# Attention and two feed-forward layers on one core: the last 512 tokens of the first phase in one group, and instruction order from a table

## The chip, the cores and the metric

The kernel runs on one core of one Trainium2 chip. The metric is the device time of one execution in microseconds (us). Five engines work from lists of their own and wait for each other by semaphores: TensorE (PE; its weight loads are shown apart as PEld), VectorE (DVE), ScalarE (ACT), GpSimd (POOL), and SyncE (SP), whose queue issues the transfers from and to memory.

## The reference

```python
scores = (1.0 / np.sqrt(D)) * np.matmul(q, k.transpose(0, 1, 3, 2))      # 2 batches, 8 heads, 768 tokens, head 64
keep = is_global | is_local                                              # first 8 tokens, or 0 <= rel < 96
scores = np.where(keep, scores + bias, -1000000000.0)                    # bias: -slope of the head * distance
a = np.exp(scores - np.max(scores, axis=-1, keepdims=True))
x = np.matmul(a / (np.sum(a, axis=-1, keepdims=True) + 1e-09), v)        # then to (1536 tokens, 512)

h = x @ moe_w_in;  x = (np.maximum(h, 0.0) + np.log1p(np.exp(-np.abs(h)))) @ moe_w_out    # 512 -> 2048 -> 512
h = x @ moe2_w_in; x = (h * np.clip(h + 3.0, 0.0, 6.0) / 6.0) @ moe2_w_out                # 512 -> 2048 -> 512
```

The weights come as 64-bit words.

## The kernel before

**Attention.** Tokens are worked on in 12 blocks of 128. A quad is half a block: four heads. Each of the 24 quads goes through scores on TensorE (`att_s`, L512, into tiles `s`), bias and minimum on VectorE (L543), exponential and row sum on ScalarE (L548), the reciprocal on VectorE (L429, L430), normalising on GpSimd (L432), eight 128x128 transposes on TensorE (`att_t`, L571, into `ptp`), copies to SBUF on ScalarE (L573, `pT`), and value matmuls on TensorE (`att_v`, L589, into `px`). Two quads make a block; then ScalarE and VectorE split the result into a high and a low part, `xsh` (L596) and `xsl` (L597). The first block of a batch has no block to its left, and its two quads have scores of 128 and not of 256 columns, half the transposes and half the value matmuls; they are called narrow here.

**The layers.** Each layer has 16 chunks of 128 hidden units, in phases of 6, 5 and 5 chunks. A chunk's product with x, the activation, and the product with the second weight matrix, summed up over a phase's chunks, are done for a group of tokens at a time. Every product is three matmuls (high by low, low by high, high by high; `matmul3`, L209). Outside the first phase a group has 512 tokens (`item`, L277: 12 matmuls into `h`, 12 into `acc`). In the first phase of the first layer, which runs beside attention, an item is a pair of chunks by 256 tokens (`first_h`, `first_o`, `first_end`; L228 to L275): a half item of 24 matmuls into `hf`, the activation (`split_g`, L184, with the tiles `t`, `ghf`, `glf`), and a half item of 24 into `accf`. There are 6 token groups of 256 and 3 pairs, so 18 items and 36 half items; `first_items` (L220) gives their order. All matmuls of the layers stand on L214.

**Weights.** A unit is half a chunk's weights (512 KB). `unit_load` (L106) loads it; `unit_convert` (L119) makes 32-bit high and low parts: from unit 12 on absolute value on ScalarE (L137) and clamp on GpSimd (L140), then always a shift (L141) and two merges (L146, L147) on VectorE, a rounding copy on ScalarE (L151), and a subtraction on VectorE (L152). The first phase uses 6 chunks, units 0 to 11. When attention is through, its memory becomes five more chunk slots (`grow`, L85), and units 12 and up are converted.

**What sets the order.** TensorE's order is written out by `run` (L368): `half` puts attention's steps in front of certain matmuls of a half item (before the first, before the thirteenth or twenty-second), and every TensorE instruction is kept in program order (`ordered`, L364). The first instruction of a unit's conversion is kept in program order too (L139, L145). All else on the other engines and the SP queue is placed by a scheduler that works with the estimated times of a simulated timeline when the program is built. Ahead of the first item TensorE does 24 warm-up matmuls (`warm_up`, L680).

Of the kernel before, what the change touches and what calls it, by code (L numbers as in the profile page):

```python
# [53 lines left out]

class Layers:
# [6 lines left out]
    def __init__(self, ctx, tc, weights, three, xsh, xsl, out):  # L62
# [14 lines left out]
        self.room, self.hint, self.bare = None, False, 0  # L77
        self.n_h, self.halves, self.in_first, self.beside = 0, 0, True, False
# [27 lines left out]
    def unit_load(self, x):  # L106
        j, u = self.order[x]
        layer, f = divmod(j, NCH)
        z = self.home(x, 5)
        if z < 2:  # L110
            raw = self.part[1][:, 2 * z:2 * z + 2, :].rearrange("p m t -> p (m t)").bitcast(I32)
            raw = raw.rearrange("p (c t) -> p c t", t=2)
        else:
            pool = self.room if z == 4 else self.wr[x % len(self.wr)]
            raw = pool.tile([P, CW, 2], I32, tag="raw", name=f"raw{j}_{u}")
        self.nc.sync.dma_start(out=raw.rearrange("p c t -> p (c t)"), in_=self.weights[2 * layer + u][f])
        self.raws[x] = raw

    def unit_convert(self, x):  # L119
# [16 lines left out]
        if not bare:  # L136
            first = nc.scalar.activation(a, raw.bitcast(F32)[:, :, 1], AF.Abs)  # L137
            if self.in_first:
                self.tc.keep_in_program_order(first)  # L139
            nc.gpsimd.tensor_scalar(out=a, in0=a, scalar1=W_HI, scalar2=W_LO, op0=ALU.min, op1=ALU.max)  # L140
        first = nc.vector.tensor_scalar(  # L141
            out=ai, in0=hi if bare else ai, scalar1=3, scalar2=0x3FFFFFF8, op0=ALU.logical_shift_left, op1=ALU.bitwise_and
        )
        if bare:
            self.tc.keep_in_program_order(first)  # L145
        nc.vector.scalar_tensor_tensor(out=ai, in0=hi, scalar=-2 ** 30, in1=ai, op0=ALU.bitwise_and, op1=ALU.bitwise_or)  # L146
        nc.vector.scalar_tensor_tensor(  # L147
            out=ai, in0=lo, scalar=29, in1=ai, op0=ALU.logical_shift_right, op1=ALU.bitwise_or
        )
        wh, wl = self.W[j][2 * u:2 * u + 2]  # L150
        nc.scalar.copy(wh, a)  # L151
        nc.vector.tensor_tensor(out=wl, in0=a, in1=r32(wh), op=ALU.subtract)  # L152
# [31 lines left out]
    def split_g(self, layer, hf, n, where=None):  # L184
# [4 lines left out]
        t3 = self.tp.tile([P, 512], F32, tag="t", name=f"t3{n}")  # L189
        if layer == 0:  # L190
            t2 = self.tp.tile([P, 512], F32, tag="t", name=f"t2{n}")
            nc.scalar.activation(t1, hf, AF.Abs)
            nc.scalar.activation(t1, t1, AF.Exp, scale=-1.0)
            if self.beside:
                nc.gpsimd.tensor_scalar(out=t2, in0=t1, scalar1=1.0, scalar2=1.0, op0=ALU.mult, op1=ALU.add)
            else:
                nc.scalar.add(t2, t1, 1.0)
            nc.scalar.activation(t3, t2, AF.Ln)
            nc.vector.scalar_tensor_tensor(out=t2, in0=t2, scalar=-1.0, in1=t1, op0=ALU.add, op1=ALU.subtract)  # L199
            nc.vector.scalar_tensor_tensor(out=t3, in0=hf, scalar=0.0, in1=t3, op0=ALU.max, op1=ALU.add)  # L200
            nc.vector.tensor_tensor(out=t3, in0=t3, in1=t2, op=ALU.subtract)
# [3 lines left out]
        nc.scalar.copy(gh, t3)  # L205
        nc.vector.tensor_tensor(out=gl, in0=t3, in1=r32(gh), op=ALU.subtract)  # L206
# [13 lines left out]
    def first_items(self):  # L220
# [4 lines left out]
        runs += [(g, EARLY_PAIRS, n) for g in range(EARLY)] + [(g, 0, n) for g in range(EARLY + 1, T // GT)]  # L225
# [38 lines left out]
    def first_end(self, i):  # L264
        g, s, _, last, more = self.items[i]
        G, o = divmod(g * GT, GB)
        if last:
            for z in range(2):
                pm = self.part[G][:, 2 * z:2 * z + 2, o:o + GT]
                if more:  # L270
                    self.nc.vector.tensor_tensor(out=pm, in0=self.acc[z], in1=pm, op=ALU.add)
                else:
                    self.nc.scalar.copy(pm, self.acc[z])
        if g == T // GT - 1:
            self.release(0, 0, (2 * s, 2 * s + 1))  # L275
# [88 lines left out]
    def ordered(self, call):  # L364

        self.tc.keep_in_program_order(call())

    def run(self, att=None, spare_step=lambda: None):  # L368
# [19 lines left out]
        grown = False  # L388
        ahead, z = [], 0
        for i in range(n):  # L390
            if not grown and (att is None or att.done()):
                if att:
                    att.close()
                    self.beside, self.room = False, None
                self.grow(1, MORE_SLOTS, 2, 2)
                grown = True
# [4 lines left out]
            self.first_end(i)  # L401
        self.in_first = False
# [24 lines left out]
def softmax_rows(nc, sm, rs, pm):  # L427

    nc.vector.tensor_scalar(out=rs, in0=sm, scalar1=EPS, scalar2=None, op0=ALU.add)  # L429
    nc.vector.reciprocal(out=rs, in_=rs)  # L430
    for j, t in enumerate(pm):
        nc.gpsimd.tensor_scalar(out=t, in0=t, scalar1=rs[:, j:j + 1], scalar2=0.0, op0=ALU.mult, op1=ALU.add)  # L432


def fast_path(tc, ident, three, nf, counts, q, k, qt, kt, v, weights, out, flag):


    with ExitStack() as ctx, ExitStack() as actx:
# [4 lines left out]
        layers.bare = 2 * PHASES[0][0]  # L443
        tp = layers.tp
# [37 lines left out]
        nc.gpsimd.iota(rel[:, 2, :], pattern=[[-1, P]], base=0, channel_multiplier=1, **iota)  # L482
        nc.gpsimd.iota(gc[:, 2, :], pattern=[[1, P]], base=0, channel_multiplier=0, **iota)
        nc.gpsimd.iota(rel[:, 1, :], pattern=[[-1, P]], base=P, channel_multiplier=1, **iota)
        nc.vector.memset(gc[:, 0:2, :], BIG)
        nc.vector.tensor_scalar(out=far[:, 2, :], in0=rel[:, 2, :], scalar1=0.0, scalar2=BIG, op0=ALU.is_lt, op1=ALU.mult)
        nc.vector.tensor_tensor(out=rel[:, 2, :], in0=rel[:, 2, :], in1=far[:, 2, :], op=ALU.add)
        nc.vector.tensor_copy(rel[:, 0, :], rel[:, 2, :])
        nc.vector.memset(rel[:, 1, 0:MAX_GLOBAL], BIG)
        nc.vector.tensor_copy(gc[:, 1, 0:MAX_GLOBAL], gc[:, 2, 0:MAX_GLOBAL])  # L490
        counts()
        ng, nl = nf[:, 0:1], nf[:, 1:2]

        nc.vector.tensor_scalar(out=gfar, in0=gc, scalar1=ng, scalar2=BIG, op0=ALU.is_ge, op1=ALU.mult)
        nc.vector.tensor_scalar(out=far, in0=rel, scalar1=nl, scalar2=BIG, op0=ALU.is_ge, op1=ALU.mult)
        nc.vector.tensor_tensor(out=far, in0=far, in1=rel, op=ALU.add)
        nc.vector.scalar_tensor_tensor(out=far, in0=gfar, scalar=nl, in1=far, op0=ALU.add, op1=ALU.min)
        for h in range(H):
# [13 lines left out]
        def att_s(k):  # L512
# [3 lines left out]
            if e == 0:  # L516
# [3 lines left out]
                if i == 0:  # L520
                    nc.scalar.copy(gk, kT[:, :, slot, 0:MAX_GLOBAL])
# [19 lines left out]
            for z in range(4):  # L541
                pmz = pm[:, z, 0:w]
                nc.vector.tensor_tensor_reduce(  # L543
# [3 lines left out]
                )  # L547
                nc.scalar.activation(pmz, pmz, AF.Exp, bias=nm[:, z:z + 1], scale=-1.0, accum_out=sm[:, z:z + 1])  # L548
# [326 lines left out]
```

## Time and profile before

| | |
|---|---|
| median of 3 runs | 631.61 us (631.17 to 632.33) |
| the profiled execution: time | 630.09 us |
| the profiled execution: span of its instructions | 628.3 us |
| TensorE busy | 613.8 us, 98% |
| VectorE, ScalarE, GpSimd busy | 71%, 60%, 21% |
| memory read and written | 56.10 MB, 3.15 MB |

The profiler records one execution. The span goes from its first to its last instruction; the 1.8 us around it belong to the time of the execution. Times in rows count from the start of the span. A matmul's recorded end is modelled and overlaps the next one's start, so what one costs in a row of many is read from the distance of the starts, or from the time of a group in the chain. The chain that ended last is followed back from the last instruction, at each step to what released it.

### The profile page before, as it was taken

Reading aid. Unit: us, or ns where it says so; the run is one execution under the profiler, and the core shown is the slowest. Engines: PE = TensorE matmul, PEld = TensorE weight load, DVE = VectorE, ACT = ScalarE, POOL = GpSimd, SP = SyncE. Lnnn points to the kernel's source line nnn. Section 1 sums busy time; section 2 is a strip of 40 time slices with the busy share of each in tenths; the row PEclk is TensorE's granted clock in tenths of the full one; section 3 lists DMA queues with packets and bytes.
Section 4 is the critical chain, followed back from the end, with each engine's and each line's share of the span. In section 5 each row is a group of like instructions: output and inputs, shape, how many; then the busy total and the mean of one; then the engine's idle time right before and its main releaser. Section 6 shows DMA issues by size and latency. Waiting matters only on the chain.

```text
span 628.3 us, 9717 instructions
## 1 busy us (share of the span) xinstructions
PE 613.8 (98%) x3495; PEld 514.8 (82%) x3496; DVE 448.8 (71%) x945; ACT 375.3 (60%) x796; POOL 132.0 (21%) x168
## 2 busy tenths in 40 slices
PE   8898999999999999999999999999999999999997
PEld 4587878899999888877788888888888888888886
DVE  7995687635799999999998996224999633424262
ACT  6986888774778887776788852425455742222130
POOL 3474353430132233533301410000100000000000
PEclk9998999999999999999999999999999999999999
DMA  8763312101144343333401143001457620001011
GB/s 278 272 196 106 106 39 69 35 14 68 68 133 137 96 139 119 123 107 117 140 34 57 45 135 101 1 1 33 142 191 233 207 67 1 1 0 68 1 67 69
DMA packets 26804, 59.91 MB, mean 95 GB/s; under 512 B 2688, under 2 KB 9344, under 8 KB 26752
## 3 DMA queue, kind: packets, MB, share of 16 engines
q1 hardware_dynamic: 26752, 59.26, 28.8%
q8 instruction: 28, 0.46, 0.3%
q14 instruction: 24, 0.20, 0.1%
HBM read 56.10 MB, written 3.15 MB: 94 GB/s over the span
## 4 chain that ended last, share of the span: by engine, by line
PE 74%; DVE 18%; ACT 4%; issue 2%; POOL 1%; DMA 0%; SPq 0%; POOLq 0%; ACTq 0%; DVEq 0%
PE acc L214 25%; PE h L214 24%; PE accf L214 8%; PE hf L214 6%; ACT pm L548 3%; PE ptp L571 2%; DVE wa L146 2%; PE accz L214 2%; PE hz L214 2%; PE px L589 2%; DVE wa L147 2%; DVE w L152 2%; PE s L537 2%; DVE t L200 1%; DVE t L199 1%
## 5 line engine op out<-in xcount | busy, mean ns | idle before, releaser
L214 PE MATMUL h<-xsh,w 128*128 128x512 f32 x584 | 154.7, 390 | 0.4 <-DVE t L200 0.4
L214 PEld LDWEIGHTS h<-xsh,w 128*128 128x128 f32 x584 | 109.1, 188 | 24.1 <-DVE t L200 1.8
L140 POOL TENSOR_SCALAR wa<-wa 128x512 f32<-128x512 f32 x52 | 67.4, 1300 | 242.7 <-ACT wa L137 242.7
L214 PE MATMUL acc<-w,gh 128*128 128x512 f32 x344 | 105.9, 389 | 0.0
L214 PE MATMUL h<-xsl,w 128*128 128x512 f32 x292 | 80.8, 389 | 0.0
L206 DVE TENSOR_TENSOR gl<-t,gh 128x512 fp32r<-128x512 f32 x73 | 51.3, 703 | 40.5 <-ACT gh L205 40.4
L214 PE MATMUL acc<-gh,w 128*128 128x512 f32 x240 | 77.7, 391 | 1.2 <-ACT gh L205 1.0
L214 PEld LDWEIGHTS acc<-w,gh 128*128 128x128 f32 x344 | 64.6, 188 | 13.5
L203 ACT ACTIVATE t<-h,three 128x512 f32<-128x512 f32 x43 | 29.5, 687 | 75.2 <-PE h L214 75.0
L204 DVE SCALAR_TENSOR_TENSOR t<-t,h 128x512 f32<-128x512 f32 x43 | 29.4, 684 | 61.4 <-ACT t L203 61.3
L432 POOL TENSOR_SCALAR pm<-pm,rs 128x256 f32<-128x256 f32 (+1 forms) x96 | 56.6, 607 | 67.5 <-DVE rs L430 31.8
L205 ACT CAST gh<-t 128x512 fp32r<-128x512 f32 x73 | 45.2, 619 | 41.4 <-PE acc L214 23.3
L214 PE MATMUL acc<-w,gl 128*128 128x512 f32 x172 | 66.9, 389 | 0.0
L214 PEld LDWEIGHTS h<-xsl,w 128*128 128x128 f32 x292 | 54.7, 188 | 11.4
L214 PE MATMUL accf<-ghf,w 128*128 128x256 f32 x288 | 58.7, 293 | 0.5 <-ACT ghf L205 0.5
L214 PEld LDWEIGHTS acc<-gh,w 128*128 128x128 f32 x240 | 44.8, 188 | 11.6 <-ACT gh L205 1.9
L548 ACT ACTIVATE pm<-pm,nm 128x256 f32<-128x256 f32 (+1 forms) x96 | 46.2, 483 | 5.6 <-DVE nm L543 5.3
L214 PEld LDWEIGHTS accf<-ghf,w 128*128 128x128 f32 x288 | 47.8, 196 | 0.9 <-ACT ghf L205 0.8
L214 PE MATMUL hf<-xsh,w 128*128 128x256 f32 x288 | 47.1, 289 | 0.0
L214 PE MATMUL acc<-gl,w 128*128 128x512 f32 x120 | 46.7, 389 | 0.0
L151 ACT CAST w<-wa 128x512 fp32r<-128x512 f32 x56 | 34.4, 615 | 17.3 <-DVE wa L147 9.6
L214 PE MATMUL accf<-glf,w 128*128 128x256 f32 x144 | 41.5, 288 | 1.5 <-DVE glf L206 1.5
(122 smaller groups left out, 1060.1 us busy)
## 6 DMA issues: line engine op xcount, KB each, us to landing
raw<-in_w2i SPq DMA_DIRECT2D x16, 512.0 KB, 3.3
raw<-in_w2o SPq DMA_DIRECT2D x16, 512.0 KB, 3.3
raw<-in_w1i SPq DMA_DIRECT2D x14, 512.0 KB, 3.8
raw<-in_w1o SPq DMA_DIRECT2D x12, 512.0 KB, 3.3
V<-in_v SPq DMA_DIRECT2D x12, 256.0 KB, 3.3
range<-in_w1i SPq DMA_DIRECT2D x6, 512.0 KB, 3.7
range<-in_w1o SPq DMA_DIRECT2D x6, 512.0 KB, 4.4
chk<-in_q SPq DMA_DIRECT2D x12, 256.0 KB, 2.7
```

What stands on the lines that cost most here:

```text
L140: nc.gpsimd.tensor_scalar(out=a, in0=a, scalar1=W_HI, scalar2=W_LO, op0=ALU.min, op1=ALU.max)
L146: nc.vector.scalar_tensor_tensor(out=ai, in0=hi, scalar=-2 ** 30, in1=ai, op0=ALU.bitwise_and, op1=ALU.bitwise_or)
L147: nc.vector.scalar_tensor_tensor(out=ai, in0=lo, scalar=29, in1=ai, op0=ALU.logical_shift_right, op1=ALU.bitwise_or)
L151: nc.scalar.copy(wh, a)
L152: nc.vector.tensor_tensor(out=wl, in0=a, in1=r32(wh), op=ALU.subtract)
L203: nc.scalar.activation(t1, hf, AF.Relu, bias=self.three[:, 0:1])
L204: nc.vector.scalar_tensor_tensor(out=t3, in0=t1, scalar=6.0, in1=hf, op0=ALU.min, op1=ALU.mult)
L205: nc.scalar.copy(gh, t3)
L206: nc.vector.tensor_tensor(out=gl, in0=t3, in1=r32(gh), op=ALU.subtract)
L214: return self.nc.tensor.matmul(out, lhsT=a, rhs=b, start=start and z == 0, stop=stop and z == len(seq) - 1, **kw)
L432: nc.gpsimd.tensor_scalar(out=t, in0=t, scalar1=rs[:, j:j + 1], scalar2=0.0, op0=ALU.mult, op1=ALU.add)
L548: nc.scalar.activation(pmz, pmz, AF.Exp, bias=nm[:, z:z + 1], scale=-1.0, accum_out=sm[:, z:z + 1])
```

## The change

The last 512 tokens of the first phase (groups 4 and 5) are no longer done in 256-column items beside the others: `first_items` leaves them out, and after attention has ended and the new slots are there, `run` does them by `item` as one group of 512 columns, chunk by chunk. So 12 items of 256 remain; attention ends among these by construction. A chunk's slot is given back as soon as that group is through with it, as in the other phases. New slots, and with them units from 12 on, now come behind the twelfth item in the program and not as soon as attention ends.

A table with one row for each of PE, ACT, DVE, POOL and SP names, in order, the instructions of attention and of the first 12 items. A label is a kind and a number, with how many of its instructions stand there: `s` scores, `t` transposes, `v` value matmuls, `Z` warm-up, `M` matmuls of the items, `e` exponentials, `T` bias and minimum, `N` normalising, `u` the VectorE steps of a unit, `w` its rounding copy, `W` its load, `A` and `L` VectorE's part of an activation, `y` the split of a block. `tie` makes each a predecessor of the next, without a semaphore. What has no label is still placed by the scheduler.

```diff
+ORDER = (
+    "Z*9 s0*3 s1*3 s0*1 s1*1 Z*4 s2*3 s3*3 s2*1 s3*1 Z*4 t0.0*1 Z*1 t0.1 t0.0*1 s4 Z*1 t1.0 t1.1*1 Z*1 t1.1*1 Z*1 "
...
+class Plan:
...
+    def mark(self, label, made):
+        self.at.setdefault(label, []).append(made.ins)
...
+        return made
+    def tie(self):
+        info = mybir.DependencyInfo(mybir.DependencyClass.NoSync, mybir.DependencyReason.DATA)
+        for row in ORDER or ():
+            last, taken = None, {}
+            for label in row.split():
...
+                for one in self.at[label][a:b]:
+                    if last is not None:
+                        self.tc.add_manual_dep(one, last.name, info, reason="order")
+                    last = one
...
     def first_items(self):
         n = PHASES[0][0] // 2
         runs = [(g, 0, EARLY_PAIRS) for g in range(EARLY)] + [(EARLY, 0, n)]
-        runs += [(g, EARLY_PAIRS, n) for g in range(EARLY)] + [(g, 0, n) for g in range(EARLY + 1, T // GT)]
+        runs += [(g, EARLY_PAIRS, n) for g in range(EARLY)] + [(g, 0, n) for g in range(EARLY + 1, (T - GB) // GT)]
...
-        if g == T // GT - 1:
-            self.release(0, 0, (2 * s, 2 * s + 1))
...
-    def ordered(self, call):
-        self.tc.keep_in_program_order(call())
+    def ordered(self, label, call):
+        made = call()
+        if self.plan:
+            self.plan.mark(label, made)
+        else:
+            self.tc.keep_in_program_order(made)
...
         for i in range(n):
-            if not grown and (att is None or att.done()):
-                if att:
-                    att.close()
-                    self.beside, self.room = False, None
-                self.grow(1, MORE_SLOTS, 2, 2)
-                grown = True
             while z <= min(i + H_AHEAD - (i < SHORT), n - 1):
                 ahead.append(h(z))
                 z += 1
             half(self.first_o(i, *ahead.pop(0)))
             self.first_end(i)
+        if att:
+            assert att.done()
+            att.close()
+            self.beside, self.room = False, None
+        if self.plan:
+            self.plan.tie()
+        self.plan, self.mark = None, lambda label, made: made
+        self.grow(1, MORE_SLOTS, 2, 2)
         self.in_first = False
         for layer in range(2):
             for ph, chunks in enumerate(PHASES[layer]):
-                if layer == 0 and ph == 0:
-                    continue
-                for G in range(T // GB):
+                for G in range(T // GB - 1 if layer == 0 and ph == 0 else 0, T // GB):
...
```

The rest of the diff gives the instructions their labels. Three places show how the order moves. Line numbers are those of the kernel each piece is from; in the changed one L214, L537, L571 are L301, L629, L665, and on VectorE L141, L146, L147, L152 are L221, L224, L227, L232, L199 to L201 and L206 are L282, L285, L288 and L293, and L543 and L597 are L635 and L691.

**Place A**, TensorE, transposes of quad 7 beside the second item's projection (`ptp7` transposes, `hf00` and `hf01` projections). Before:

```order
L571 MATMUL ptp7_0_731<-ident_59,pm7_552 128x128 x4
L214 MATMUL hf01_2_696<-xsh0_75,w1_2_361 128x256 x4
L214 MATMUL hf01_2_696<-xsl0_78,w0_2_360 128x256 x4
L214 MATMUL hf01_2_696<-xsh0_75,w0_2_360 128x256 x4
L214 MATMUL hf01_2_696<-xsh0_75,w1_3_423 128x256 x4
L214 MATMUL hf01_2_696<-xsl0_78,w0_3_422 128x256 x4
L214 MATMUL hf01_2_696<-xsh0_75,w0_3_422 128x256
L571 MATMUL ptp7_1_759<-ident_59,pm7_552 128x128 x4
```

and in the change:

```order
L301 MATMUL hf00_1_549<-xsh0_75,w0_1_306 128x256 x3
L665 MATMUL ptp7_0_731<-ident_59,pm7_552 128x128
L301 MATMUL hf00_1_549<-xsh0_75,w0_1_306 128x256
L665 MATMUL ptp7_0_731<-ident_59,pm7_552 128x128
L301 MATMUL hf01_2_696<-xsh0_75,w1_2_361 128x256
L665 MATMUL ptp7_0_731<-ident_59,pm7_552 128x128
L301 MATMUL hf01_2_696<-xsh0_75,w1_2_361 128x256
L665 MATMUL ptp7_0_731<-ident_59,pm7_552 128x128
L301 MATMUL hf01_2_696<-xsh0_75,w1_2_361 128x256 x2
```

The block of four transposes became four single ones with a matmul between each two.

**Place B**, VectorE, bias and minimum of quads 5 and 6 (each `ISA` with a read of its minimum behind it; `part2` and `w1` are weights being converted, `xsl0` is a block's low part). Before:

```order
L543 ISA pm5_433,nm5_434<-s5_1_432,bias_142 128x256
L543 ISA nm5_434 128x1
L152 TENSOR_TENSOR w1_2_361<-part2_92,w0_2_360 128x512
L146 SCALAR_TENSOR_TENSOR part2_92<-raw3_0_292,part2_92 128x512
L147 SCALAR_TENSOR_TENSOR part2_92<-part1_91,part2_92 128x512
L430 RECIPROCAL rs4_391<-rs4_391 128x4
L543 ISA pm6_494,nm6_495<-s6_0_492,bias_142 128x256
L543 ISA nm6_495 128x1
L543 ISA pm6_494,nm6_495<-s6_0_492,bias_142 128x256
L543 ISA nm6_495 128x1
L147 SCALAR_TENSOR_TENSOR part2_92<-raw3_0_292,part2_92 128x512
L543 ISA pm6_494,nm6_495<-s6_1_493,bias_142 128x256
```

and in the change:

```order
L635 ISA pm5_433,nm5_434<-s5_1_432,bias_142 128x256
L635 ISA nm5_434 128x1
L691 TENSOR_TENSOR xsl0_78<-px0_340,xsh0_75 128x4x128
L224 SCALAR_TENSOR_TENSOR part2_92<-part1_91,part2_92 128x512
L635 ISA pm6_494,nm6_495<-s6_0_492,bias_142 128x256
L635 ISA nm6_495 128x1
L635 ISA pm6_494,nm6_495<-s6_1_493,bias_142 128x256
L635 ISA nm6_495 128x1
L635 ISA pm6_494,nm6_495<-s6_0_492,bias_142 128x256
L635 ISA nm6_495 128x1
L635 ISA pm6_494,nm6_495<-s6_1_493,bias_142 128x256
L635 ISA nm6_495 128x1
```

Weight steps that stood between and among the scores of quads 5 and 6 now come later.

**Place C**, VectorE at the end of attention, in the change (`wa` units from 12 on, `t3f11` and `glf11` the activation of the last 256-column item, `xsl2` from `px11` the last block of attention):

```order
L285 SCALAR_TENSOR_TENSOR t3f11_2185<-hf32_12_2157,t3f11_2185 128x512
L227 SCALAR_TENSOR_TENSOR wa7_0_2445<-raw7_0_2335,wa7_0_2445 128x512
L232 TENSOR_TENSOR w1_6_2340<-wa6_0_2343,w0_6_2339 128x512
L288 TENSOR_TENSOR t3f11_2185<-t3f11_2185,t2f11_2186 128x512
L232 TENSOR_TENSOR w1_7_2442<-wa7_0_2445,w0_7_2441 128x512
L221 TENSOR_SCALAR wa6_1_2392<-wa6_1_2392 128x512
L293 TENSOR_TENSOR glf11_2183<-t3f11_2185,ghf11_2182 128x512
L691 TENSOR_TENSOR xsl2_80<-px11_2031,xsh2_77 128x4x128
L224 SCALAR_TENSOR_TENSOR wa6_1_2392<-raw6_1_2333,wa6_1_2392 128x512
L221 TENSOR_SCALAR wa7_1_2494<-wa7_1_2494 128x512
```

Three units are under way ahead of the last block's split; before, the first of them came behind it.

## Rows read from the trace of the kernel before

**Rows 1.** The page: busy us of TensorE, its share of the span, instructions.

```profile
PE 613.8 (98%) x3495; PEld 514.8 (82%) x3496; DVE 448.8 (71%) x945; ACT 375.3 (60%) x796; POOL 132.0 (21%) x168
```

**Rows 2.** Busy time by stretch: us, then each engine's busy us, granted clock, DMA.

```profile
20.00:40.00 20.00, 16.86 (x152) 12.83 (x150) 19.87 (x66) 17.37 (x55) 10.87 (x17) 1.00 0.67 219
40.00:60.00 20.00, 18.01 (x154) 15.59 (x153) 15.07 (x47) 15.41 (x43) 9.69 (x15) 0.91 0.39 123
...
100.00:120.00 20.00, 20.00 (x186) 17.79 (x185) 14.37 (x52) 17.21 (x52) 8.94 (x16) 1.00 0.14 47
```

**Rows 3.** Waits of TensorE, 140 us to the end: total us, times, longest.

```profile
PE acc L214 <- ACT gh L205: 1.0, 2, 0.8
PE h L214 <- DVE t L200: 0.4, 1, 0.4
```

**Rows 4.** Waits of TensorE, 0 to 32.4 us.

```profile
PE ptp L571 <- POOL pm L432: 1.9, 4, 0.5
PE px L589 <- ACT pT L573: 1.4, 2, 1.0
PE warm L683 <- DVE zeros L458: 1.3, 1, 1.3
PE s L537 <- DVE nm L543: 0.3, 1, 0.3
```

**Rows 5.** Waits of TensorE, 32.4 to 100 us.

```profile
PE ptp L571 <- ACT pT L573: 2.1, 3, 1.0
PE accf L214 <- DVE glf L206: 1.5, 1, 1.5
PE accf L214 <- ACT ghf L205: 0.5, 1, 0.5
```

**Rows 6.** The chain that ended last: start us, us, what and how many.

```profile
51.18 4.15 PE accf L214 x20
...
64.36 2.51 PE accf L214 x21
...
144.43 3.06 PE hf L214 x24
...
173.41 2.88 PE hf L214 x24
...
304.19 2.72 PE acc L214 x12
```

**Rows 7.** Timeline of TensorE: start us, us to the modelled end, what.

```profile
67.61 0.71 PE L537 MATMUL s<-kT,qT 64*128 64x128 f32 x8
...
99.83 0.72 PE L214 MATMUL hf<-xsh,w 128*128 128x256 f32 x4
...
102.43 0.60 PE L571 MATMUL ptp<-ident,pm 128*128 128x128 f32 x4
102.78 0.60 PE L214 MATMUL hf<-xsh,w 128*128 128x256 f32 x3
103.31 1.13 PE L537 MATMUL s<-kT,qT 64*128 64x256 f32 x8
...
105.81 0.36 PE L214 MATMUL accf<-ghf,w 128*128 128x256 f32 x1
```

**Rows 8.** Groups of TensorE's instructions: busy us, mean ns, idle before.

```profile
L683 PE MATMUL warm<-zeros 128*128 128x512 bf16 x23 | 8.2, 512 | 1.5 <-DVE zeros L458 1.3 <-issue 0.2
```

**Rows 9.** Timeline of VectorE beside the conversions.

```profile
179.15 0.41 DVE L141 TENSOR_SCALAR wa<-wa 128x512 int32<-128x512 int32 x1
179.49 0.68 DVE L146 SCALAR_TENSOR_TENSOR wa<-raw,wa 128x512 int32<-128x512 int32 x1
180.09 0.68 DVE L199 SCALAR_TENSOR_TENSOR t2f<-t2f,t1f 128x512 f32<-128x512 f32 x1
```

**Rows 10.** Timeline of the SP queue.

```profile
144.52 0.80 SPq L116 DMA_DIRECT2D raw<-in_w1o  x2
```

**Rows 11.** Issues of transfers: how many, size, median us to landing.

```profile
raw<-in_w1o SPq DMA_DIRECT2D x12, 512.0 KB, 3.3
```

More of the change, by code (lines that the diff above doesn't have):

```diff
@@ L115, in unit_load @@
             raw = pool.tile([P, CW, 2], I32, tag="raw", name=f"raw{j}_{u}")
-        self.nc.sync.dma_start(out=raw.rearrange("p c t -> p (c t)"), in_=self.weights[2 * layer + u][f])
+        self.mark(f"W{x}", self.nc.sync.dma_start(
+            out=raw.rearrange("p c t -> p (c t)"), in_=self.weights[2 * layer + u][f]
+        ))
         self.raws[x] = raw
@@ L136, in unit_convert @@
         if not bare:
[L137 to L139 removed]
+            nc.scalar.activation(a, raw.bitcast(F32)[:, :, 1], AF.Abs)
             nc.gpsimd.tensor_scalar(out=a, in0=a, scalar1=W_HI, scalar2=W_LO, op0=ALU.min, op1=ALU.max)
[L141 removed]
+        self.mark(f"u{x}.0", nc.vector.tensor_scalar(
             out=ai, in0=hi if bare else ai, scalar1=3, scalar2=0x3FFFFFF8, op0=ALU.logical_shift_left, op1=ALU.bitwise_and
[L143 to L147, printed above, removed]
+        ))
+        self.mark(f"u{x}.1", nc.vector.scalar_tensor_tensor(
+            out=ai, in0=hi, scalar=-2 ** 30, in1=ai, op0=ALU.bitwise_and, op1=ALU.bitwise_or
+        ))
+        self.mark(f"u{x}.2", nc.vector.scalar_tensor_tensor(
             out=ai, in0=lo, scalar=29, in1=ai, op0=ALU.logical_shift_right, op1=ALU.bitwise_or
[L149 removed]
+        ))
         wh, wl = self.W[j][2 * u:2 * u + 2]
[L151 to L152 removed]
+        self.mark(f"w{x}", nc.scalar.copy(wh, a))
+        self.mark(f"u{x}.3", nc.vector.tensor_tensor(out=wl, in0=a, in1=r32(wh), op=ALU.subtract))
     def range_step(self, x, m):
@@ L204, in split_g @@
             nc.vector.scalar_tensor_tensor(out=t3, in0=t1, scalar=6.0, in1=hf, op0=ALU.min, op1=ALU.mult)
-        nc.scalar.copy(gh, t3)
-        nc.vector.tensor_tensor(out=gl, in0=t3, in1=r32(gh), op=ALU.subtract)
+        mark(f"h{n}", nc.scalar.copy(gh, t3))
+        mark(f"L{n}", nc.vector.tensor_tensor(out=gl, in0=t3, in1=r32(gh), op=ALU.subtract))
         return gh, gl
@@ L481, in fast_path @@
         iota = dict(allow_small_or_imprecise_dtypes=True)
[L482 to L486, printed above, removed]
@@ L551, in att_s @@
             rs = ap_m.tile([P, 4], F32, tag="rs", name=f"rs{k}")
-            softmax_rows(nc, sm, rs, [pm[:, z, 0:w] for z in range(4)])
+            softmax_rows(nc, sm, rs, [pm[:, z, 0:w] for z in range(4)], lambda label, made: mark(f"{label}{k}", made))
             if e == KC // 2 - 1 and 1 <= i < NB - 1:
-                nc.scalar.copy(kT[:, :, slot, 0:MAX_GLOBAL], gk)
+                mark(f"r{k}", nc.scalar.copy(kT[:, :, slot, 0:MAX_GLOBAL], gk))
             pms[k] = pm
@@ L682, in warm_up @@
             for _ in range(m):
-                layers.ordered(lambda: nc.tensor.matmul(warm, lhsT=zeros[:, 0:P], rhs=zeros, start=True, stop=True))
+                layers.ordered("Z", lambda: nc.tensor.matmul(warm, lhsT=zeros[:, 0:P], rhs=zeros, start=True, stop=True))
         warm_up(WARM)
```

123 lines of the change are left out of this document (75 added, 48 removed), and 46 rows, old and new, of the table ORDER.

## The prediction

> **What bounds the kernel now.** I read the busy times first, then their course over time, then what TensorE waited for, then its single instructions.
>
> The page has TensorE busy 98% of the span [rows 1]. The stretches of 20 us [rows 2] show where that hides something: from 20 to 60 us TensorE is at 17 to 18 of 20 while VectorE is at 19.9 and then 15, ScalarE at 17.4 and 15.4; from 100 us on TensorE is full. So the first 100 us, attention beside the first phase, are set by a chain through several engines, and what follows by TensorE; its waits from 140 us to the end are 1.0 and 0.4 us and smaller [rows 3]. The reader is to see two things: an instruction saved on TensorE after 100 us is time saved; before that, mostly a wait saved is.
>
> What TensorE waits for early: up to 32.4 us, where the first projection matmul stands, POOL's normalised rows 1.9 us, copies on ScalarE 1.4, scores' buffers 0.3, and 1.3 at the start [rows 4]; from there to 100 us copies 2.1, the activation 1.5 and 0.5 [rows 5]. There is a price beside the wait. Behind the two waits on the activation, 20 matmuls of 256 columns took 4.15 us, where 21 took 2.51 later [rows 6]: 1.7 us, and the mean granted clock of that stretch is 0.91 [rows 2], so for some of it the lower of the two levels (1.2, not 2.4 GHz) was granted.
>
> **The change, part by part.** Every sum is against the profiled execution (span 628.3 us, time 630.09 us; the median of the runs shown is 631.61 us, 1.5 us above it).
>
> *Wider matmuls.* Six items of 256 columns (groups 4 and 5, three chunk pairs) become six chunks of 512. Removed: 6 x 48 = 288 matmuls, 24 of which take 2.88 us one after the other, 120 ns each. Added: 144, 12 of which take 2.72 us, 227 ns each [rows 6]. 288 x 0.120 - 144 x 0.227 = 34.6 - 32.6 = 1.9 us saved, with rounding; TensorE is full there, so all of it lies on the path. The six activations are 128x512 in both, and four copies of sums replace four.
>
> The Trainium skill ("TensorE: Matmul & The Clock Gate", Back-to-back issue gap) gives a warm matmul N/2.4 ns plus 2.5. By that the saving would be an estimated 0.4 us and not 1.9, and the forecast 1.5 us later. The rows have about 13 ns above the columns' time at either width, so I keep the rows.
>
> *The table.* It adds no instruction; it moves them, and holds each engine to its list up to the end of the twelve items of 256 columns. So I compare TensorE's work to the end of the first phase with the time it had.
>
> - One half item with a wide quad takes 5.98 us where TensorE is full (99.83 to 105.81) [rows 7]. Less its 24 matmuls (2.88) the quad costs 3.10; 20 quads, 62 us. In the four narrow ones (a batch's first block) scores take 0.71 and not 1.13 us [rows 7]; by that share 2.0 us each, 8 together.
> - The warm-up is 8.2 us busy [rows 8] and the start 1.3 us [rows 4], in both.
> - Before: 62 + 8 + 8.2 + 1.3 = 79.5 us, and 18 half items (51.8) by the end of attention: 131.3. It ended at 144.4 [rows 6], so 13.1 us were waits and half clock. 18 half items follow: the first phase is through after 196.2 us of its own (the next phase's matmuls that are put between only change places).
> - After: the table has 510 of the 576 narrow matmuls ahead of the last value matmul (61.2 us), 66 behind it (7.9), then the wide ones (32.6): 79.5 + 61.2 + 7.9 + 32.6 = 181.2 us, plus the waits W.
>
> So the change is W - 15.0 us. With W as before, 13.1, only the 1.9 is left.
>
> *What W will be.* The waits up to 32.4 us are 3.6 us without the start. Projection matmuls still come only behind quad 8's scores, so nothing new can fill these: W is at least 3.6. The other 9.5 us lie between 32 and 100 us, and there the table acts twice. Place A in the section on the change: four transposes stood together, and now stand singly between projection matmuls, so a late slice holds up less. Place B: VectorE, full from 20 to 40 us, now does quad 6's scores with no weight work among them. I count 23 weight operations ahead of quad 8's last score before and 13 now; at 0.60 us (0.34 for the one shift among the ten; spacing in [rows 9]) 5.7 us less stand ahead of it. That work comes back ahead of quad 10, where about 2 us less are left. I take it that two thirds of the 9.5 go: W = 3.6 + 3.2, about 7. Bounds: 3.6, and 13.1 or more (rivals).
>
> *Behind attention.* The second phase's weights are converted only from here, and now beside fewer matmuls (7.9 + 32.6 us for 51.8). Place C: the subtraction glf11, which the last 24 narrow matmuls need, stands on VectorE behind the shift of wa6_1. Its load was issued right at the end of attention before (144.52) [rows 10], and a load takes 3.3 us to land [rows 11]; with Abs, clamp, shift and glf11 (0.6, 0.6, 0.3 and 0.7, sizes as in [rows 9]) glf11 is done some 5.6 to 6 us after attention, and TensorE needs it after 42 x 0.12 = 5.0. I charge 1.0 us. From there VectorE's list has 83 operations up to the activation of the second phase's first item: 69 x 0.60 + 14 x 0.34 = 46.2 us [rows 9]. It begins them 6.5 us after attention and is through at 52.7. TensorE gets there after 66 x 0.12, five projections of 12 x 0.227 and 144 x 0.227 more: 7.9 + 13.6 + 32.6 = 54.1. So they are covered, by 1.4 us. If that cover is gone, see rival 2. The waits that TensorE has later [rows 3] I leave as they are.
>
> Sum: 7 - 15.0 + 1.0 = -7.0 us. From 631.6, **624.6 us**.
>
> **Rivals.**
>
> 1. *The waits stay* (W about 13): the chain of scores, exponential, normalising, transpose and copy is as long as before, and single transposes only spread it. For it: VectorE and ScalarE are both near full between 20 and 40 us. Against: ten operations fewer ahead of quad 8. 13.1 - 15.0 + 1.0 = -0.9: 630.7 us.
> 2. *VectorE becomes the bound of the 512-column items.* Its cover is 1.4 us out of 53. If an operation comes every 0.68 us (its busy time in [rows 9]) and not every 0.60, 69 x 0.08 = 5.5 us are added, 4.1 past the cover: 628.7 us. Against: before, with the same kind of list, TensorE's waits from 140 us on are small [rows 3].
> 3. *The fixed lists stall the engines, and it gets slower.* In a list an instruction whose operand is late holds up all that stands behind it. Place: ScalarE's and VectorE's lists up to 100 us, where quads are mixed more finely than before. It decides from W = 14. Were the named waits (3.6 and 4.1 us) doubled, W = 20.8 and the change is +6.8: 638.4 us. Against: from 35 us on TensorE's list always has narrow matmuls beside what may be late. The Trainium skill (the same page, Architectural detail) calls ScalarE's and VectorE's queues strictly first in, first out, which speaks against an order named by hand; no row of this case tests it, and the lists before were as fixed.
> 4. *Going from a matmul to a transpose and back costs.* I count 57 such changes before and 204 now. Three matmuls behind four transposes took 0.53 us (102.78 to 103.31) and not 0.36 [rows 7]; were these 0.17 the price of a pair of changes and not of the scores behind, 147 x 0.085 = 12.5 us are added, so +5.5: 637.1 us. It decides from 48 ns a change. Against: the 0.53 us have the change to the scores' other shape in them.
>
> **How the numbers follow.** My forecast (W from 3.6 to 10, so 621 to 628 us): 0.55. Rival 1: 0.11. Rival 2: 0.16. Rival 3: 0.12. Rival 4: 0.06. The range begins at 618 us (W at its lower bound, no stall behind attention, and the later waits of 1.4 us gone too: 618.8) and goes to 633, beyond rivals 1 and 2; it leaves out rivals 3 and 4. A measurement tells 0.2%, 1.3 us, from no change. Faster by more: forecast, rival 2 and a little of rival 1, 0.73. Within it: most of rival 1, 0.09. Slower: rivals 3 and 4, 0.18.
>
> **What would show it.** Right: the last value matmul at about 148 us (79.5 + 61.2 + 7), the first wide accumulation some 22 us later, the clock of 40 to 60 us near 1.0, TensorE's waits for pT and the activation halved. Wrong in W: the last value matmul at 153 us or later. Rival 2: TensorE idle on gl or gh between 165 and 210 us. Rival 4: 24 narrow matmuls with eight transposes among them take clearly over 2.88 + 0.9 us with no idle time.

## The result, and the profile after

The changed kernel takes **623.02 us** (median of 4 runs, 622.42 to 624.31), the kernel before 631.39 us (median of 4). The ratio is 0.9863, with a 95% interval from 0.9842 to 0.9884: 8.4 us faster, 7.3 to 10.0 by the interval. Forecast were 624.6 us and -7.0. The profiled execution took 622.77 us with a span of 621.0 us, 7.3 us less than before.

The page's busy times, to hold against [rows 1]:

```profile
PE 611.2 (98%) x3350; PEld 507.4 (82%) x3352; DVE 447.7 (72%) x945; ACT 375.0 (60%) x795; POOL 136.2 (22%) x169
```

TensorE's share is 98% as before; this row doesn't tell where the time went. The stretches do (columns as in [rows 2]), and TensorE's waits behind them, first 0 to 32.4 us, then 32.4 to 100 us, then 140 us to the end:

```profile
20.00:40.00 20.00, 19.52 (x186) 15.78 (x183) 18.81 (x62) 18.65 (x54) 14.17 (x21) 1.00 0.65 218
40.00:60.00 20.00, 20.00 (x189) 17.91 (x188) 18.84 (x62) 17.39 (x51) 9.60 (x14) 1.00 0.46 161
...
140.00:160.00 20.00, 19.64 (x155) 17.99 (x154) 19.49 (x37) 13.02 (x24) 6.74 (x8) 1.00 0.49 176
160.00:180.00 20.00, 19.55 (x84) 15.04 (x83) 19.07 (x32) 16.38 (x29) 4.86 (x6) 1.00 0.40 136
```

```profile
PE warm L777 <- DVE zeros L550: 1.3, 1, 1.3
PE s L629 <- DMA qT<-in_qt: 0.6, 1, 0.6
PE ptp L665 <- ACT pm L640: 0.3, 1, 0.3
PE ptp L665 <- ACT pT L667: 0.2, 1, 0.2
...
PE s L629 <- DVE rs L517: 0.3, 1, 0.3
...
PE acc L301 <- DVE gl L293: 1.3, 2, 0.7
PE h L301 <- DVE t L285: 0.8, 2, 0.6
PE accf L301 <- DVE glf L293: 0.4, 1, 0.4
PE acc L301 <- ACT gh L292: 0.2, 1, 0.2
```

From 20 to 60 us TensorE is busy 39.5 of 40 us, where it was 34.9 [rows 2], and the granted clock from 40 to 60 us is 1.00 where it was 0.91. The named waits of 3.6 and 4.1 us ahead of 100 us [rows 4, 5] are down to 1.1 (without the start) and 0.3. From 140 us on it is the other way: the waits were 1.6 us, all between 270 and 301 us [rows 3], and are 2.7. Of these, 0.8 lie between 152 and 176 us, where VectorE is nearly full (19.49 and 19.07 of 20), 0.6 at 242 us, and 1.3 at 498 and 502 us.

I keep the prediction's W: the time at which the last value matmul starts, less 79.5 us and less 0.12 us for each of the narrow matmuls ahead of it. Before it is 144.15 - 79.5 - 51.8 = 12.8 us, now 145.15 - 79.5 - 61.2 = **4.5 us**. The end of attention on TensorE, before and then in the change (each time the last value matmuls, `px`, and the matmul behind them):

```profile
143.33 1.09 PE L589 MATMUL px<-pT,V 128*64 128x128 f32 x16
144.36 0.74 PE L214 MATMUL hf<-xsh,w 128*128 128x256 f32 x4
```

```profile
143.46 1.97 PE L683 MATMUL px<-pT,V 128*64 128x128 f32 x32
145.35 0.39 PE L301 MATMUL accf<-ghf,w 128*128 128x256 f32 x1
```

The fall of 8.3 us in W is nearly all accounted for: the named waits went from 7.7 to 1.4 us, 6.3 less, and the 1.7 us that the prediction put down to slow matmuls behind two waits [rows 6] are gone with the clock of 0.91. TensorE's loss elsewhere, called excess below, I take from the distances of the starts, above 120 and 227 ns a matmul:

| part | us |
|---|---|
| W, 12.8 to 4.5 | -8.3 |
| wider matmuls | -1.9 |
| new excess, 152 to 203 us (behind attention) | +2.3 |
| excess 264 to 301 us before (3.2), 230 to 243 us now (1.4) | -1.8 |
| new excess, 497 to 502 us | +1.8 |
| sum (the span fell by 7.3) | -7.9 |

The parts overshoot the span by 0.6 us, which I can't place.

### The profile page after: what moved, and what is told of

The parts are those of the page before. It is cut to its first block, busy times and chain, and to the rows that moved or that the text cites. A ratio compares the mean times of both kernels' runs of the same rounds, so it can differ in the third digit from the quotient of the medians.

```text
span 621.0 us, 9444 instructions
## 1 busy us (share of the span) xinstructions
PE 611.2 (98%) x3350; PEld 507.4 (82%) x3352; DVE 447.7 (72%) x945; ACT 375.0 (60%) x795; POOL 136.2 (22%) x169
## 4 chain that ended last, share of the span: by engine, by line
PE 66%; DVE 18%; DMA 8%; ACT 4%; issue 3%; POOL 0%; SPq 0%; ACTq 0%; POOLq 0%
PE acc L301 23%; PE h L301 21%; PE hf L301 5%; PE accf L301 3%; PE s L629 3%; PE px L683 3%; PE ptp L665 3%; DVE wa L227 3%; DVE wa L224 3%; PE accz L301 2%; DMA chk<-in_q 2%; DMA chk<-in_k 2%; PE hz L301 2%; DVE w L232 2%; DVE gl L293 2%
## 5 line engine op out<-in xcount | busy, mean ns | idle before, releaser
L301 PE MATMUL h<-xsh,w 128*128 128x512 f32 x632 | 167.3, 390 | 0.9 <-DVE t L285 0.8
L301 PEld LDWEIGHTS h<-xsh,w 128*128 128x128 f32 x632 | 118.0, 188 | 27.3 <-DVE t L285 3.1
L301 PE MATMUL acc<-w,gh 128*128 128x512 f32 x344 | 106.0, 389 | 0.0
L301 PE MATMUL acc<-gh,w 128*128 128x512 f32 x288 | 92.0, 390 | 0.2 <-ACT gh L292 0.2
L293 DVE TENSOR_TENSOR gl<-t,gh 128x512 fp32r<-128x512 f32 x79 | 55.0, 696 | 48.4 <-ACT gh L292 48.3
L301 PE MATMUL h<-xsl,w 128*128 128x512 f32 x316 | 86.7, 389 | 0.0
L301 PEld LDWEIGHTS acc<-w,gh 128*128 128x128 f32 x344 | 64.6, 188 | 13.4
L291 DVE SCALAR_TENSOR_TENSOR t<-t,h 128x512 f32<-128x512 f32 x43 | 29.4, 684 | 55.9 <-ACT t L290 55.8
L301 PEld LDWEIGHTS h<-xsl,w 128*128 128x128 f32 x316 | 59.2, 188 | 12.4
L301 PE MATMUL acc<-w,gl 128*128 128x512 f32 x172 | 67.2, 391 | 1.3 <-DVE gl L293 1.3
L520 POOL TENSOR_SCALAR pm<-pm,rs 128x256 f32<-128x256 f32 (+1 forms) x96 | 57.0, 609 | 43.6 <-DVE rs L518 25.4
L301 PEld LDWEIGHTS acc<-gh,w 128*128 128x128 f32 x288 | 53.9, 188 | 12.4 <-ACT gh L292 1.0
L301 PE MATMUL acc<-gl,w 128*128 128x512 f32 x144 | 56.0, 389 | 0.0
L219 ACT ACTIVATE wa<-raw 128x512 f32<-128x512 f32 x52 | 35.0, 673 | 14.6 <-DVE w L232 6.0
L635 DVE CUSTOM_DVE_ANT_0 pm<-s,bias 128x256 f32<-128x256 f32 (+1 forms) x96 | 35.1, 394 | 10.2 <-PE s L629 9.9
L301 PE MATMUL accf<-ghf,w 128*128 128x256 f32 x192 | 41.8, 299 | 0.0
L232 DVE TENSOR_TENSOR w<-wa,w 128x512 fp32r<-128x512 f32 x56 | 38.8, 695 | 3.3 <-ACT w L231 3.3
```

What stands on the lines that cost most here:

```text
L232: self.mark(f"u{x}.3", nc.vector.tensor_tensor(out=wl, in0=a, in1=r32(wh), op=ALU.subtract))
L291: nc.vector.scalar_tensor_tensor(out=t3, in0=t1, scalar=6.0, in1=hf, op0=ALU.min, op1=ALU.mult)
L293: mark(f"L{n}", nc.vector.tensor_tensor(out=gl, in0=t3, in1=r32(gh), op=ALU.subtract))
L301: return self.nc.tensor.matmul(out, lhsT=a, rhs=b, start=start and z == 0, stop=stop and z == len(seq) - 1, **kw)
L520: mark("N", nc.gpsimd.tensor_scalar(out=t, in0=t, scalar1=rs[:, j:j + 1], scalar2=0.0, op0=ALU.mult, op1=ALU.add))
L635: mark(f"T{k}.{z}", nc.vector.tensor_tensor_reduce(out=pmz, in0=ps[z % 2][:, z // 2, 0:nsl, :].rearrange("p s t -> p (s t)"), in1=bias[:, ...
```

## The experiments

Each is an edit of the changed kernel ("the change"), except where said, in 5 to 12 runs, with before measured beside it (its medians 631.6 to 631.8 us).

**Both parts alone.** E1 sets the table to nothing:

```diff
-ORDER = (
...
+ORDER = None
```

> The 512-column group stays, the table is taken out (each engine but TensorE is again placed by the scheduler, TensorE in program order). Theory (the table takes TensorE's waits out of attention, the wide group gives 1.9 us alone): W is back at about 13 us, the last value matmul some 8.6 us later for the matmuls ahead of it than with the table, and the time lies 1 to 2 us below the kernel before, at 629.5 to 630.5 us. Rival (the wide group, and that the second phase's weights then start later, gives most of it): 626 us or less. Clock of 40 to 60 us back near 0.91 by the theory, near 1.0 by the rival.

Measured: 630.84 us, ratio 0.9985 (0.9968 to 1.0002); W 13.2 us, clock from 40 to 60 us 0.91. The row of 40 to 60 us:

```profile
40.00:60.00 20.00, 17.98 (x153) 15.55 (x152) 15.06 (x47) 15.52 (x43) 9.73 (x15) 0.91 0.38 123
```

The theory holds in W and clock, with a time 0.3 us above its range: without the table nothing is left of W's gain, and the wide group alone brings 0.9 us in the medians, with an interval that just reaches no change.

E2 keeps the table and puts the last 512 tokens behind it in six narrow items; `late_narrow` is a loop of `first_h`, `first_g`, `first_o` and `first_end` over groups 4 and 5:

```diff
-                for G in range(T // GB - 1 if layer == 0 and ph == 0 else 0, T // GB):
+                if layer == 0 and ph == 0:
+                    self.late_narrow()
+                    continue
+                for G in range(T // GB):
```

> The table stays with its twelve items, and the last 512 tokens go back to six items of 256 columns behind it. Theory: 288 matmuls at 120 ns for 144 at 227 ns, so 1.9 us more than the change, 624.9 us; attention as in the change (last value matmul at 145 us). By the Trainium skill's issue gap (TensorE: Matmul & The Clock Gate) it would be an estimated 0.4 us. Rival (the narrow items hide more of VectorE's weight work, or the wide ones stall on it): the same time as the change or less, 623 us or below.

Measured: 622.37 us, ratio 0.9841 (0.9825 to 0.9856), against 0.9842 to 0.9884 of the change: no difference that the intervals show. The forecast of 1.9 us more missed, and the rival held. The waits of this run from 140 us on:

```profile
PE h L301 <- DVE t L285: 0.9, 1, 0.9
PE acc L301 <- DVE gl L293: 0.4, 1, 0.4
```

1.3 us where the change has 2.7, none of them between 152 and 203 us, and the excess of 2.3 us there is gone (0.3 left from 140 to 200 us). From 203 to 246 us E2 has 2.3 us of excess and the change 1.5, around 500 us it has 0.7 and the change 1.8, and its W is 1.5 us higher (6.0). With the 1.9 us of the matmuls that makes -2.3 + 0.8 - 1.1 + 1.5 + 1.9 = 0.8 us, and its span is 0.7 us longer (621.7 against 621.0). So the wide matmuls may well have saved their 1.9 us and lost them again behind attention; E11 and E12 settle it.

**Which rows of the table.** E3 to E7 tie only some engines' rows and leave the others to the scheduler (in E3 the first VectorE operation of a unit is kept in program order, as before; in E4 to E7 nothing outside the tied rows is). This is E4's edit, rows 0 and 2 being TensorE's and VectorE's:

```diff
-        for row in ORDER or ():
+        for row in [ORDER[z] for z in (0, 2)]:
```

> Only TensorE's row of the table is tied; VectorE, ScalarE, GpSimd and SyncE go back to the scheduler, which puts 20 weight operations ahead of quad 8's last score (13 in the change, 23 before). Theory (Place A, the mixed order on TensorE, and Place B, weight work out of the scores' way, both carry it): about half of the 8.6 us in W is given back, 626 to 628 us, VectorE's scores of quad 8 some 4 us later than in the change. If TensorE's order alone carries it: 623 to 624 us. If VectorE's order carries it alone: 630 us.

> TensorE's and VectorE's rows are tied, those of ScalarE, GpSimd and SyncE are not. Theory: the two rows carry the gain, 623 to 624.5 us, W at 5 to 6 us. Rival (it takes all rows, since ScalarE is nearly full between 20 and 40 us too): 626 us or more.

> Four rows tied, ScalarE's left to the scheduler. With TensorE's and VectorE's rows alone TensorE waited 3.3 us on ScalarE's pT, 1.8 on GpSimd's pm and 1.4 on the load of V up to 100 us. Theory (a row is worth what the rows of the engines that feed it agree with; ScalarE, nearly full between 20 and 40 us, is the one that was missing): 628 to 632 us, W from 11 to 15 us. Rival (GpSimd's and SyncE's rows were missing): 623 to 625 us.

> The rows of TensorE, ScalarE and VectorE tied, GpSimd's and SyncE's left to the scheduler: the counterpart of the run without ScalarE's row. Theory (ScalarE's row was missing): 623 to 625.5 us, W from 4.5 to 7. Rival (GpSimd's and SyncE's rows carry it): 628 us or more.

> Four rows tied, VectorE's left to the scheduler, which puts 20 weight operations ahead of quad 8's last score (13 in the change, 23 before). Theory (Place B: 7 operations of 0.60 us more ahead of the scores, 4.2 us, which TensorE's list then waits for): 627 us or more, W at 9 or more. Rival (VectorE's order matters little as long as the others are tied): 623 to 625 us.

| run | rows tied | W, us | median, us | ratio, 95% |
|---|---|---|---|---|
| E1 | none | 13.2 | 630.84 | 0.9968 to 1.0002 |
| E3 | TensorE | 25.4 | 643.37 | 1.0163 to 1.0194 |
| E4 | TensorE, VectorE | 14.9 | 632.18 | 0.9991 to 1.0011 |
| E7 | all but VectorE | 23.9 | 644.16 | 1.0180 to 1.0247 |
| E5 | all but ScalarE | 12.8 | 634.73 | 1.0030 to 1.0071 |
| E6 | TensorE, ScalarE, VectorE | 8.3 | 627.38 | 0.9911 to 0.9957 |
| change | all five | 4.5 | 623.02 | 0.9842 to 0.9884 |

W is read from one execution each; in E3 and E7 that one took 2.7 and 3.7 us less than the median.

All three forecasts for E3 fell (623 to 630 us): TensorE's new order by itself makes the kernel 11.7 us slower than before. E4's theory fell too, its rival held. E5 is above its theory's range: W is as expected (12.8), but 3.8 of the 12.1 us that its span is longer than the change's come from elsewhere; its distances have more excess behind 140 us too. E6 fell between its two forecasts: GpSimd's and SyncE's rows are worth 3.8 us of W, ScalarE's 8.3 (E5 against the change), so both theories had a part. In E7 the theory's sign held, and its size was far too small. The waits from 32.4 to 100 us show the mechanism, E3 first, then E7:

```profile
PE ptp L665 <- ACT pT L667: 5.1, 6, 1.8
PE px L683 <- DMA V<-in_v: 1.0, 1, 1.0
PE px L683 <- ACT pT L667: 0.8, 1, 0.8
PE hf L301 <- DVE xsl L691: 0.7, 1, 0.7
```

```profile
PE ptp L665 <- POOL pm L520: 3.4, 2, 2.2
PE accf L301 <- DVE glf L293: 2.1, 1, 2.1
PE px L683 <- ACT pT L667: 2.1, 1, 2.1
PE accf L301 <- ACT ghf L292: 1.5, 1, 1.5
```

TensorE stands at an instruction whose operand is late, and all narrow matmuls behind it in its list stand too. In E7 only 2.1 of the 9.1 us name VectorE, the engine whose row was taken out; up to 32.4 us another 3.3 us name its minimum. Its last score operation of quad 10 starts at 58.0 us (47.3 in the change), and what ScalarE and GpSimd make of these scores follows late.

**Place A undone.** E8 ties all rows, with the transposes of a half quad together again at the place of the first:

```diff
-    ... "t7.0*1 M*1 t7.0*1 M*1 t7.0*1 M*1 t7.0*1 M*7 t7.1*1 M*1 ..."
+    ... "t7.0 M*1 M*1 M*1 M*7 t7.1 M*1 ..."
```

> All rows tied, but in TensorE's the transposes of a half quad stand together again, at the place of the first of them: 68 changes between matmul and transpose instead of 204 (57 before). Place A (a block waits as a whole for the latest slice): 2 to 4 us slower than the change, 625 to 627 us, TensorE's waits for pm and pT up to 100 us at 2 us or more. Rival 4 (each change costs 0.085 us): 136 x 0.085 = 11.6 us faster, 611 us. Neither: within 1 us of the change.

Measured: 626.65 us, ratio 0.9914 (0.9885 to 0.9943), 3.6 us above the change, W 9.9 us. The waits of 0 to 32.4 and of 32.4 to 100 us that name pm:

```profile
PE ptp L623 <- POOL pm L478: 0.7, 1, 0.7
...
PE ptp L623 <- POOL pm L478: 1.4, 2, 1.0
```

E8 came out as forecast for Place A, and rival 4 is refuted by 15 us. E8 doesn't show the block's own price, though: the other four rows stay tied to lists that were made for single transposes, and E3 to E7 show what lists cost that don't fit. The change's own timeline says the same as E8 of the price of going to and fro:

```profile
104.15 0.28 PE L665 MATMUL ptp<-ident,pm 128*128 128x128 f32 x1
104.18 0.37 PE L301 MATMUL hf<-xsh,w 128*128 128x256 f32 x1
104.38 0.38 PE L665 MATMUL ptp<-ident,pm 128*128 128x128 f32 x2
104.52 0.36 PE L301 MATMUL hf<-xsh,w 128*128 128x256 f32 x1
104.72 0.27 PE L665 MATMUL ptp<-ident,pm 128*128 128x128 f32 x1
104.75 0.48 PE L301 MATMUL hf<-xsh,w 128*128 128x256 f32 x2
105.07 0.64 PE L301 MATMUL hf<-xsl,w 128*128 128x256 f32 x4
```

From 104.15 to 105.07 four transposes and four matmuls start, with five changes between them: 0.92 us, and 4 x 0.120 leave 0.11 for a transpose. In a block before, single starts lie 0.109 us apart (102.43, 102.53, 102.64 and 102.75 us), so a transpose costs no more by itself. The 0.17 us that rival 4 was built on split into 0.08 that belong to the block's last transpose (the first matmul behind it starts after 0.03 us, the second only 0.20 later) and 0.09 for the change to the scores' shape (0.21 and not 0.12 us).

**What was left behind attention.** Two stalls seemed to be order and not load. Between 497 and 502 us ScalarE's copies gh stand behind squares of the spare check steps that wait for their loads: both t that are copied at 497.27 and 500.96 us were done by 495.14 us (VectorE's L291). The timeline of ScalarE and of TensorE in the change:

```profile
500.33 0.63 ACT L747 ACTIVATE chk<-chk 128x512 f32<-128x512 f32 x1 [0.84 <-DMA chk<-in_k]
500.87 0.18 ACT L747 ACTIVATION_READ_ACCUMULATOR chk<-chk 128x1 f32 x1
500.96 0.60 ACT L292 CAST gh<-t 128x512 fp32r<-128x512 f32 x1
...
502.35 0.50 PE L301 MATMUL acc<-w,gl 128*128 128x512 f32 x1 [0.66 <-DVE gl L293]
```

And VectorE's list behind attention has conversions between the steps of an activation: L282 of the first wide item at 163.83 us, its L288 only at 166.99, with a merge, a subtraction and a shift of weights between. E9 ties each square behind its item's gh, E10 a unit's first VectorE operation behind the gl of the item before last, E11 does both, and E12 both with E2's narrow items. `behind` sets an order without a semaphore, as `tie` does; `last` holds the items' gh and gl so far, and the second `made` is the shift of `unit_convert`:

```diff
-            nc.scalar.activation(x, x, AF.Square, accum_out=sq[:, t:t + 1])
+            made = nc.scalar.activation(x, x, AF.Square, accum_out=sq[:, t:t + 1])
+            layers.behind(made, layers.last["gh"][-1])
...
+        if x >= 12 and len(self.last["gl"]) > 1 and not self.in_first:
+            self.behind(made, self.last["gl"][-2])
```

> As the change, but each square of the spare check steps (ScalarE) is tied behind the copy gh of the item it belongs to, so that they are spread over the items, where in the change they stand close together from 485 to 503 us and the copies gh behind squares that wait for their load. Theory (the 1.8 us that TensorE loses between 497 and 502 us come from there): 621 us, no excess interval between 480 and 520 us. Rival (they come from VectorE or the loads themselves): 622.5 to 623.5 us.

> As the change, but from unit 12 on the first VectorE operation of a unit is tied behind the subtraction gl of the item before last, so the scheduler can no longer put conversions ahead of the activation on VectorE's list. Theory (the 2.3 us lost between 152 and 203 us, and the 1.4 between 230 and 243, are order and not VectorE's throughput): 620 to 621.5 us. Rival (VectorE is the bound there, and pacing only moves the wait): 622.5 us or more.

> Checks tied and units paced together. If both theories hold the savings add up: 618.5 to 620 us; if only the checks hold: 621 us.

> Checks tied and units paced, but with the last 512 tokens in 256-column items behind the table. Theory (the 1.9 us of the wide matmuls were made in the change and given back as waits on VectorE): with those waits gone the narrow group is 1.9 us slower than the run with both, 620.5 to 622 us. Rival (the wide matmuls save nothing): the same time as with both.

| run | median, us | ratio, 95% | span, us | W, us |
|---|---|---|---|---|
| E9 checks tied | 621.43 | 0.9822 to 0.9869 | 619.6 | 6.0 |
| E10 units paced | 619.60 | 0.9798 to 0.9841 | 617.7 | 4.6 |
| E11 both | **616.60** | 0.9754 to 0.9802 | 614.6 | 4.1 |
| E12 both, narrow group | 619.58 | 0.9798 to 0.9840 | 616.7 | 4.1 |

E9 came out at its theory, E10 and E12 0.4 and 0.9 us below their ranges. E11 is 1.9 us below its range: the excess that it takes away (1.8, 2.3 and 1.4 us) adds up to 5.5, and 6.4 us are gone where I had counted on 3 to 4.5. E9 has no excess from 480 to 520 us; by the intervals it can't be told from the change, since they overlap, so E9 alone rests on its trace. E10 has none from 160 to 500 us; 2.6 us at the check steps, which it doesn't touch, remain. E11 has neither, and from 140 us on its trace names no wait of TensorE at all. It beats both kernels: 15.2 us below before, 6.4 below the change. VectorE in E10 behind attention shows why pacing works:

```profile
153.93 0.69 DVE L236 TENSOR_TENSOR w<-wa,w 128x512 fp32r<-128x512 f32 x1 [0.69 <-ACT w L235]
160.44 0.69 DVE L286 SCALAR_TENSOR_TENSOR t<-t,t 128x512 f32<-128x512 f32 x1 [5.82 <-ACT t L285]
161.05 0.68 DVE L289 SCALAR_TENSOR_TENSOR t<-h,t 128x512 f32<-128x512 f32 x1
161.77 0.69 DVE L292 TENSOR_TENSOR t<-t,t 128x512 f32<-128x512 f32 x1
```

VectorE now idles 5.82 us ahead of the first wide activation, and TensorE waits less: the wait behind attention was one of order, and not of VectorE's throughput. E12 against E11, with the same W and no waits to speak of on either side, is the price of the wide group: 2.1 us in the spans (0.4 of it excess in E12 at 220 to 240 us), 3.0 in the medians, for 1.9 forecast. The Trainium skill ("TensorE: Matmul & The Clock Gate", Back-to-back issue gap) gave an estimated 0.4. It states its formula for an isolated matmul, and its figure of 2.5 ns above the columns' time isn't what these rows, a stream of matmuls, have (about 13).

## Why the prediction was right, point by point

- **Sign and size held** (-7.0 forecast, -8.4 measured, inside the range; -7.3 between the profiled executions). The ground was right: attention was set by a chain, the table took TensorE's waits out of it, and E1 shows that without it the gain is gone. That the sum is so close is in part luck: W came out 2.5 us better than forecast and the stretch behind attention 1.3 us worse.
- **W was mis-sized**: 7 forecast, 4.5 measured, by two steps. "W is at least 3.6" held the waits up to the first projection fixed because nothing new could fill them. They fell from 3.6 to 1.1 us all the same, and all that stands ahead of the first projection runs earlier: it starts at 27.77 us, and started at 32.42 (there ahead of quad 8's scores, at 34.64 us, and not behind them, as I wrote).

```profile
27.77 0.74 PE L301 MATMUL hf<-xsh,w 128*128 128x256 f32 x4
```

  And "two thirds of the 9.5 go" was too little for what lies behind: the named waits there fell from 4.1 to 0.3 us. That W still ends above 3.6 doesn't save the bound, since only 1.4 of the 4.5 us are named waits; the other 3.1 are in no wait, as were some 3.4 before (12.8 less 7.7 and 1.7). The last value matmul started at 145.2 us, not 148, and the first wide accumulation 23.2 us later (22 forecast); clock (1.00) and the halved waits came as written.
- **Place A held in sign**: undone, it costs 3.6 us in the medians (E8). How much of that is the block, and how much the other rows that no longer fit, isn't shown. **Place B held in sign only**: VectorE's last score operation of quad 8 starts at 29.9 us, 37.6 before, and without VectorE's row W is 23.9 (E7). But by the operations ahead of a score I expected 4.2 us of such an order, and E7 lost 19.4 us of W. With no row tied at all W is 13.2 (E1), so 10.7 of these come only with the other four rows, which were made to fit VectorE's.
- **What I left out**: the prediction argued from two engines' lists. E4 shows that these two alone give 632.2 us, nothing; ScalarE's row is worth 8.3 us of W and GpSimd's and SyncE's 3.8. The worth of the rows doesn't add up; it belongs to lists that agree. The other four rows beside TensorE's old program order were not tried.
- **The wider matmuls' 1.9 us** were right as a term (E12 against E11). In the change they are not in the time, since the stalls behind attention took 2.3 us where I had charged 1.0.
- **Behind attention** the place was right (glf11 behind the shift of wa6_1: VectorE's glf at 152.25 us), the size not: TensorE waited 0.36 us there. Both sides of the sum were too short, and nearly alike: glf was done 7.8 us after attention and not 5.6 to 6, and TensorE came to it after 7.5 us and not 5.0. Eight wide projection matmuls among the narrow ones are 1.8 us of that.

```profile
151.50 0.83 DVE L221 TENSOR_SCALAR wa<-wa 128x512 int32<-128x512 int32 x1 [0.51 <-POOL wa L220]
152.25 0.68 DVE L293 TENSOR_TENSOR glf<-t3f,ghf 128x512 fp32r<-128x512 f32 x1
...
156.94 0.68 DVE L232 TENSOR_TENSOR w<-wa,w 128x512 fp32r<-128x512 f32 x1
157.54 0.68 DVE L224 SCALAR_TENSOR_TENSOR wa<-raw,wa 128x512 int32<-128x512 int32 x1
158.14 0.68 DVE L232 TENSOR_TENSOR w<-wa,w 128x512 fp32r<-128x512 f32 x1
...
152.97 0.39 PE L301 MATMUL accf<-glf,w 128*128 128x256 f32 x1 [0.36 <-DVE glf L293]
```

- The 54.1 us of cover held as a sum: TensorE's trace names no wait between 176 and 242 us. It said that VectorE's work fits, not that each activation comes in time: the other 2 us behind attention are of that kind. The step "the waits that TensorE has later I leave as they are" failed both ways (-1.8 and +1.8 us) and came out even by luck.
- **Rivals.** 1 (waits stay) is what E1 and E5 look like in W, not the change. 2 had the right engine and the wrong reason: VectorE's operations still start every 0.60 us (156.94, 157.54, 158.14 above) and not every 0.68. TensorE stalls on single operands (glf, t, gh) for 2.3 us and not 4.1, of its sign (idle on gl or gh between 165 and 210 us) there are 0.17 us, and E10 takes the stalls away with VectorE idle in between. 3 did not happen in the change, and is real: E3 and E7 are 11.7 and 12.6 us slower than before, more than its 6.8, with the waits that it describes. It takes only lists that don't fit each other. In the change's own trace a square that waited for its load held up the copy gh behind it on ScalarE. The Trainium skill's rule of strict first in, first out ("TensorE: Matmul & The Clock Gate", Architectural detail) agrees with that. 4 is refuted (E8).

## What to carry to other kernels

Here an order table paid most as a whole: TensorE's row alone, or all rows but VectorE's, cost some 12 us against the scheduler's own order, while three rows of five (E6) kept half of the gain. So change and measure lists together with the lists that feed them. When a sum says that an engine's work fits under another's, ask also in which order it does it: tying background work behind the step that the bound engine waits for gave 6.4 us more here, with no instruction saved.

## What the runs showed that I had not expected

- The same early scores have two speeds. From TensorE's timeline in the change, and then in E9, whose lists are the same there:

```profile
6.62 1.01 PE L629 MATMUL s<-kT,qT 64*128 64x128 f32 x12 [0.63 <-DMA qT<-in_qt]
```

```profile
6.78 1.78 PE L638 MATMUL s<-kT,qT 64*128 64x128 f32 x12 [0.73 <-DMA qT<-in_qt]
```

  12 scores take 1.01 or 1.78 us, though the granted clock reads 1.00 in both and the wait ahead is about as long (E10, E11 and E12, with 1.0, 1.15 and 1.1 us, have the fast form). E2, E8 and E9 have the slow form. W is 6.0 in E2 and E9, and 4.1 to 4.6 in the four runs with all rows tied and the fast form. So of the 5.4 us by which E8's W is above the change's, 1.5 may belong to this, and 3.9 to the blocks of transposes. What decides it stays open.
- The granted clock doesn't follow the total of the waits in these two executions: between 32.4 and 100 us E3 waited 8.3 us and has 1.00 in every stretch of 20 us; E7 waited 9.1 us, and had 0.97 from 40 to 60 us and 0.86 from 60 to 80 us, where three waits of 1.5 to 2.2 us lie between 53 and 63 us.
